# Joined score matmuls in chunks 1 to 3, and a new order of all steps, in a transformer block on one core

## The chip, the cores and the metric

The kernel runs on one core of a Trainium2 chip. A core has five engines that work side by side, each through its own queue in order: TensorE (PE, matmuls; its weight loads are shown apart as PEld), VectorE (DVE), ScalarE (ACT), GpSimd (POOL) and SyncE (SP). Here POOL and SP mostly issue DMA transfers. The metric is the device time of one execution in microseconds; lower is better.

## The reference

One transformer block over 2048 positions of width 512 in bf16. The attention has 32 heads of width 16; each position looks at eight keys, at distances 0, 2, ..., 14 behind it. A feed-forward with a gate, ReLU and width 1376 follows.

```python
off = jnp.arange(8) * 2
idx = pos[:, None] - off[None, :]
mask = idx >= 0
kg = k[:, :, idx_c, :]; vg = v[:, :, idx_c, :]
logits = jnp.einsum("bhsd,bhswd->bhsw", q, kg) * Dh ** -0.5
attn = softmax(where(mask, logits, -1e9))
o = jnp.einsum("bhsw,bhswd->bhsd", attn, vg)

h  = x + attention(layernorm(x)) @ wo
gate = layernorm(h) @ W_gate
up = layernorm(h) @ W_up
h2 = h + (gate * (gate > 0) * up) @ W_down
```

## The kernel before

The 2048 positions go in four chunks (0 to 3) of 512, each of four blocks of 128. Per chunk:

- **Layer norm and projections.** DVE takes statistics, DVE or ACT normalizes, PE (or a DMA transposition on SP, L533) transposes each block, ACT copies it out of PSUM (L560, for pairs of blocks; in chunk 0 block 1's copy is DVE's). Twelve groups of four matmuls (L585) give q, k and v; ACT evicts each (L593).
- **Scores.** The channels are laid out so that a score is a product of q with a shifted k, summed over channels. The eight shifts go in two halves of four (`hf` 0 and 1). DVE multiplies q with shifted k (L636; L651 in chunk 0), two products per half, each 128 x 4096, into the buffers `big`. PE then sums over channels with matmuls whose weights have only 32 columns, so that four of them, one for each shift, use the array together (`tile_position`). A half is one PE step, `sc0` or `sc1`, and one PSUM bank: 16 matmuls (L642), or 8 (L694) where DVE has added the two products first (L680: chunk 2's second half and both halves of chunk 3). ACT takes the exponential of each bank (L708).
- **Attention output.** DVE adds the two halves' exponentials (`es`, L740), PE sums them (`den`, L725), ACT makes the reciprocal, DVE scales the exponentials (L752; in chunk 0 it is done at the end). DMAs on SP and POOL spread them over the channels (`bd`, L768). DVE multiplies with shifted v (`mu`, L800; L815 in chunk 0) and sums eight terms: the first fold by an accumulating DMA on POOL (`ta`, L843) except in one case, the others on DVE (`tree`, L803, L837; `om`, L807). PE does the output projection (`wo`, L881), DVE adds it to x (`rs`, L892).
- **Feed-forward.** ACT squares for the variance (L457), DVE normalizes (`hxn`, L510), four DMA transpositions on SP (`htd`, L533), then up and gate groups of four matmuls (L954), ACT evicts (L958, L961), DVE multiplies (`gu`, L982). The last 96 of the 1376 channels go transposed (L921, L927, L931, and a DMA transposition, L940). PE does the down projection in two parts for each block (`dn`, L1005). In chunks 0 and 1 ACT scales the result (L1011), a DMA on POOL adds it into `x_sm` (`oa`, L1034) and SP stores it (`os`, L1037); in chunks 2 and 3 DVE adds (L1013) and SP stores (L1019), the very last store goes from ACT's queue.

All of this is a list of steps. `add` gives each step its engine, an estimated length, the steps it waits for and the buffers it takes. `RANK` holds one number for each step: the steps are placed in the order of these numbers, so they fix the order of every engine's queue. `Plan.order` also estimates when each step starts, from the arrival times `XT` and `WT` of the loads and the lengths (`MM`, `SW`, ...), and takes for each buffer the one that it thinks is free first. What runs on the chip is the queues in that order, with the waits that the data need. The matmuls of one step stand together in PE's queue.

Buffers that matter here: eight PSUM banks for all results of PE, five `big` buffers of 128 x 4096 (a sixth, the place of the q and k weights, once the last projection has read them) for products, spread weights and value products.

The load of the up weights (`ldu`, L315, two halves) waits for a small DVE copy behind chunk 0's attention (`lg`, L861). The gate weights are loaded in `setup` (L349).

Of the kernel before, what the change touches and what calls it, by code (L numbers as in the profile page):

```python
# [8 lines left out]
P = 128  # L9
# [3 lines left out]
ACT = mybir.ActivationFunctionType  # L13
ALU = mybir.AluOpType
# [3 lines left out]
RANK = [  # L18
# [38 lines left out]
]  # L57
# [36 lines left out]
class Plan:  # L94
# [9 lines left out]
    def add(self, key, *a, **k):  # L104
        op = Op(*a, **k)
        op.key = key
        op.seq = len(self.ops)
        if RANK:
            op.prio = RANK[op.seq]
        self.ops.append(op)  # L110
        for b in set(op.take) | set(op.use):
            b.left += 1
        return op
# [88 lines left out]
def kernel(  # L202
# [11 lines left out]
    nc = tc.nc  # L214
# [8 lines left out]
    PADL = 16  # L223
# [6 lines left out]
    LATE = "ud"  # L230
    NAB = 0
    SCALE = DH ** -0.5
# [68 lines left out]
    V = nc.vector  # L301
# [4 lines left out]
    def f_load(n, i):  # L306
        if n == "d":
            lo, hi = (0, 5) if i == 0 else (5, NFF)
            nc.sync.dma_start(
                wd_sb[:, lo:hi, :], B_W_down[lo * P:hi * P, :].rearrange("(ft p) n -> p ft n", p=P))  # L310
            if FTAIL and i:
                nc.sync.dma_start(wd_sb[:FTAIL, NFF, :], B_W_down[NFF * P:F, :])
        else:
            w = B_W_up.rearrange("(dt p) f -> p dt f", p=P)
            nc.sync.dma_start(wgu_sb[:, 2 * i:2 * i + 2, 1, :], w[:, 2 * i:2 * i + 2, :])  # L315

    def setup():
# [30 lines left out]
        nc.sync.dma_start(wo_sb[:], A_wo.rearrange("(p t) f -> p t f", t=NT))  # L348
        nc.sync.dma_start(wgu_sb[:, :, 0, :], B_W_gate.rearrange("(dt p) f -> p dt f", p=P))  # L349


# [15 lines left out]
    add = plan.add  # L367
# [11 lines left out]
    QA, QC = 6, 3  # L379
    XT = (3.45, 3.65, 4.05, 5.3, 7.15, 8.65, 9.0, 9.4, 13.0, 14.5)  # L380
    WT = (8.35, 8.35, 7.0, 10.85, 15.8, 25.5, 19.2, 29.0)
    DMAT = (('h',0,0),('h',0,2),('h',2,0),('h',2,2),('h',3,0),('h',3,2),('h',1,0),('h',1,2),('x',3,0),('x',3,2))
# [7 lines left out]
    MERGE = (0, 1, 2, 3)  # L390

    BCN = 4

    HG = ([[0, 1, 2, 3]],) * 4
    HSP = ()
    XG = ([[0], [1], [2], [3]], [[0, 1, 2, 3]], [[0, 1, 2, 3]], [[0, 1, 2, 3]])
    TMT = (0, 1, 2, 3)
    TTM, DTG, ATE = 0.0825, 0.27, 0.225
    LASTC = (D // 2, 3 * D // 4)
# [4 lines left out]
    MM, TP = 0.2158, 0.056  # L404
    SW = 0.21
    PEL = 0.22
# [22 lines left out]

    fills = [add(("warm", 0), "PE", 5.6, f_warm, [], -500, take=[wb])]  # L430

    def fill(d, k):
# [7 lines left out]
    def layernorm(tk, src, dst_slots, pr, groups, on_act, residual=None):  # L440
# [7 lines left out]
        for grp in groups:  # L448
# [78 lines left out]
            for j0 in range(lo, hi, step):  # L527
# [23 lines left out]

                tev = not residual and tk == 0 and j0 == 1

# [14 lines left out]
    for tk in range(NCK):  # L568
# [51 lines left out]
        kd = {t: kdone[tk, t] for t in range(NT)}  # L620
        kp = {t: kdone.get((tk - 1, t)) for t in range(NT)}
        for hf in range(2):
            sc, ex = Buf(at_s), Buf(ex_s)
# [54 lines left out]
            elif (tk, hf) in PRE:  # L678
# [18 lines left out]

                scd = [add(("sc%d" % hf, tk), "PE", nu * MM + SW, f_sc, [a], apr, take=[sc], use=[prd[0][1]], lat=PEL)]
            elif tk in MERGE:
# [6 lines left out]

            def f_ex(sc=sc, ex=ex):
                nc.scalar.activation(out=ex.t[:], in_=sc.t[:], func=ACT.Exp, scale=SCALE)  # L708

            def f_mk(hf=hf, ex=ex):  # L710
                V.tensor_tensor(out=ex.t[:, 0:PADL], in0=ex.t[:, 0:PADL], in1=mask[:, hf, :],
                                op=ALU.mult)

            a = add(("ex%d" % hf, tk), "ACT", A5, f_ex, scd, apr, take=[ex], use=[sc], lat=AL)
            if tk == 0:
                a = add(("mk%d" % hf, tk), "DVE", DSM, f_mk, [a], apr, use=[ex], lat=DL)
            exs.append(ex)
            exd.append(a)

# [139 lines left out]
        if tk == 0 and LATE:  # L859
            def f_lg(OT=OT):  # L860
                V.tensor_copy(out=wgu_sb[0:1, :, 1, 0:1], in_=OT.t[0:1, :, 0:1])  # L861

            lg = add(("lg", tk), "DVE", 0.08, f_lg, list(oev.values()), apr, use=[OT], lat=0.1)
            for n in LATE:
                for i in range(2):
                    wload[n].append(add(("ld" + n, i), "SP", 0.45 + 0.1 * (n == "d" and i), lambda n=n, i=i: f_load(n, i),
                                        [lg], 0, lat=1.0 + 1.0 * (n == "d" and i), dq=(1.0, 1.74)))
# [227 lines left out]
```

## Time and profile before

| what | us |
|---|---|
| median of three runs | 191.26 |
| lowest and highest run | 191.16, 192.79 |
| span of the profiled execution | 190.2 |
| PE busy in it | 185.1 |
| DVE busy | 150.7 |
| ACT busy | 113.5 |
| POOL busy | 25.2 |

All times in the views are from the start of that span. A matmul's record is longer than its share of PE's time, because matmuls overlap in the array: one of 512 columns is recorded with 379 ns. What a row of PE's timeline costs is read from its start to the start of the next row. The clock granted to PE over the span is 0.998 of full speed. "To landing" is the time from a DMA's issue to the arrival of its data.

### The profile page before, as it was taken

Reading aid. Unit: us, or ns where it says so; the run is one execution under the profiler, and the core shown is the slowest. Engines: PE = TensorE matmul, PEld = TensorE weight load, DVE = VectorE, ACT = ScalarE, POOL = GpSimd, SP = SyncE. Lnnn points to the kernel's source line nnn. Section 1 sums busy time; section 2 is a strip of 40 time slices with the busy share of each in tenths; the row PEclk is TensorE's granted clock in tenths of the full one; section 3 lists DMA queues with packets and bytes.
Section 4 is the critical chain, followed back from the end, with each engine's and each line's share of the span. In section 5 each row is a group of like instructions: output and inputs, shape, how many; then the busy total and the mean of one; then the engine's idle time right before and its main releaser. Section 6 shows DMA issues by size and latency. Waiting matters only on the chain.

```text
span 190.2 us, 3080 instructions
## 1 busy us (share of the span) xinstructions
PE 185.1 (97%) x1127; PEld 95.4 (50%) x1127; DVE 150.7 (79%) x231; ACT 113.5 (60%) x234; POOL 25.2 (13%) x47
## 2 busy tenths in 40 slices
PE   7799999999999999999999999999999999999993
PEld 7676555554444445544344464444454444455453
DVE  5899999999999999999999998998485712114324
ACT  2579999985467945762483795146466713358500
POOL 4000221400000004230033123027000000000000
PEclk9999999999999999999999999999999999999999
DMA  5999364993198858998438798779922211000503
GB/s 182 281 347 370 90 163 87 191 194 59 21 330 177 233 166 153 194 191 182 83 65 152 142 181 186 180 137 166 221 44 55 55 28 59 28 0 0 165 3 110
DMA packets 27743, 26.98 MB, mean 142 GB/s; under 512 B 14704, under 2 KB 23248, under 8 KB 27728
## 3 DMA queue, kind: packets, MB, share of 16 engines
q1 hardware_dynamic: 23696, 15.34, 29.7%
q0 software_dynamic: 3312, 10.49, 28.6%
q10 hardware_dynamic: 720, 0.95, 1.5%
q8 instruction: 9, 0.15, 0.3%
q14 instruction: 6, 0.05, 0.1%
HBM read 8.42 MB, written 2.10 MB: 55 GB/s over the span
## 4 chain that ended last, share of the span: by engine, by line
PE 82%; ACT 11%; DMA 3%; DVE 1%; issue 1%; SPq 0%
PE bank L954 37%; PE bank L1005 20%; PE bank L585 12%; PE bank L881 7%; ACT row L512 5%; DMA x_sm<-in_A_x_dram 3%; PE bank L921 3%; ACT quad L560 2%; ACT vT L593 2%; PE bank L642 2%; ACT quad L593 1%; PE bank L694 1%; ACT kT L593 1%; ACT ex L708 1%; SPq L323 0%
## 5 line engine op out<-in xcount | busy, mean ns | idle before, releaser
L954 PE MATMUL bank<-quad,wgu_sb 128*128 128x512 bf16 x320 | 72.3, 379 | 0.0
L954 PEld LDWEIGHTS <-wgu_sb 128*128 128x128 bf16 x320 | 30.9, 98 | 37.3 <-issue 1.7
L1005 PE MATMUL bank<-wd_sb,gT 128*128 128x512 bf16 (+3 forms) x198 | 39.7, 355 | 0.0
L958 ACT CAST up_sb<-bank 128x512 bf16<-128x512 f32 x40 | 23.1, 591 | 21.0 <-PE bank L954 14.9
L585 PE MATMUL bank<-quad,wqk_sb 128*128 128x512 bf16 (+2 forms) x176 | 30.4, 321 | 0.5 <-DVE quad L558 0.4
L961 ACT ACTIVATE gr<-bank 128x512 bf16<-128x512 f32 x40 | 23.3, 606 | 9.7 <-PE bank L954 8.2
L1005 PEld LDWEIGHTS <-gT 128*128 128x128 bf16 (+1 forms) x198 | 18.5, 98 | 19.7
L982 DVE TENSOR_TENSOR gT<-gr,up_sb 128x1024 bf16<-128x1024 bf16 x20 | 13.6, 686 | 14.4 <-PE bank L1005 7.0
L636 DVE TENSOR_TENSOR big<-quad,kT 128x4096 bf16<-128x4096 bf16 x11 | 24.8, 2279 | 0.0
L585 PEld LDWEIGHTS <-wqk_sb 128*128 128x128 bf16 x176 | 17.1, 113 | 11.4 <-issue 1.1
L800 DVE TENSOR_TENSOR big<-big,vT 128x4096 bf16<-128x4096 bf16 x9 | 20.4, 2281 | 0.0
L843 POOL DMA_DIRECT2D big<-big x13 | 11.6, 965 | 64.3 <-PE bank L954 32.6
L1013 DVE SCALAR_TENSOR_TENSOR row<-bank,iv,x_sm 128x512 bf16<-128x512 f32 (+2 forms) x10 | 6.3, 643 | 13.4 <-PE bank L1005 13.2
L457 ACT ACTIVATE junk<-x_sm,sm 128x512 bf16<-128x512 bf16 x16 | 11.6, 727 | 8.8 <-DVE x_sm L892 8.8
L585 PE MATMUL bank<-quad,wv_sb 128*128 128x512 bf16 x64 | 16.1, 380 | 0.2 <-ACT quad L560 0.2
L881 PE MATMUL bank<-wo_sb,quad 128*128 128x512 bf16 x64 | 15.0, 379 | 0.0
L892 DVE SCALAR_TENSOR_TENSOR x_sm<-x_sm,bank 128x512 bf16<-128x512 bf16 x16 | 10.8, 678 | 2.4 <-PE bank L881 2.4
L803 DVE TENSOR_TENSOR big<-big 128x1024 bf16<-128x1024 bf16 (+1 forms) x17 | 10.3, 622 | 1.6 <-DMA big<-big 1.4
L467 DVE BATCH_NORM_STATS2 st<-x_sm 128x6 f32<-128x512 bf16 x16 | 10.2, 679 | 1.1 <-DMA x_sm<-in_A_x_dram 1.1
L593 ACT CAST quad<-bank 128x512 bf16<-128x512 f32 x16 | 9.3, 594 | 2.5 <-PE bank L585 2.4
L593 ACT CAST kT<-bank 128x512 bf16<-128x512 f32 x16 | 9.3, 596 | 1.9 <-PE bank L585 1.0
L593 ACT CAST vT<-bank 128x512 bf16<-128x512 f32 x16 | 9.1, 610 | 2.1 <-PE bank L585 2.1
(80 smaller groups left out, 175.6 us busy)
## 6 DMA issues: line engine op xcount, KB each, us to landing
big<-big POOLq DMA_DIRECT2D x13, 512.0 KB, 5.2
big<-ex SPq DMA_DIRECT2D x20, 128.0 KB, 3.1
big<-ex POOLq DMA_DIRECT2D x12, 128.0 KB, 3.8
wgu_sb<-in_B_W_gate_dram SPq DMA_DIRECT2D x1, 1376.0 KB, 9.3
wgu_sb<-in_B_W_up_dram SPq DMA_DIRECT2D x2, 688.0 KB, 5.0
wd_sb<-in_B_W_down_dram SPq DMA_DIRECT2D x2, 640.0 KB, 5.7
x_sm<-in_A_x_dram SPq DMA_DIRECT2D x2, 512.0 KB, 6.2
wqk_sb<-wqk_sb POOLq DMA_DIRECT2D x2, 512.0 KB, 5.8
```

Source lines behind the costliest of these rows:

```text
L457: nc.scalar.activation(out=junk[:, j % 2, :], in_=h.t[:] if h else x_sm[:, tk * BPC + j, :], func=ACT.Square, bias=sm.t[:, j:j + 1], scale ...
L585: nc.tensor.matmul(mm.t[:, lo:hi], lhsT=wv_sb[:, dt, t:D:NT] if c == 2 else wqk_sb[:, dt, c * D + t:(c + 1) * D:NT], rhs=xnT.t[:, dt, lo:h ...
L593: nc.scalar.copy(out=o, in_=mm.t[:])
L636: V.tensor_tensor(out=pb.t[:].rearrange("p (t w) s -> p t w s", t=2), in0=q4, in1=k4, op=ALU.mult)
L800: V.tensor_tensor(out=mt.t[:], in0=ab.t[:], in1=v8, op=ALU.mult)
L843: nc.gpsimd.dma_start(mt.t[:, 0:4, :], mt.t[:, 4:8, :], accum_op=ALU.add)
L881: nc.tensor.matmul(od.t[:], lhsT=OT.t[:, t, j * P:(j + 1) * P], rhs=wo_sb[:, t, :], start=(t == 0), stop=(t == NT - 1 and tk not in RPE))
L954: nc.tensor.matmul(mm.t[:fs, lo:hi], lhsT=wgu_sb[:, dt, g, ft * P: ft * P + fs], rhs=hnT.t[:, dt, lo:hi], start=(dt == 0), stop=(dt == NT ...
L958: nc.scalar.copy(out=ub.t[:fs, i, :], in_=um.t[:fs, :])
L961: nc.scalar.activation(out=gr.t[:fs, i, :], in_=gm.t[:fs, :], func=ACT.Relu)
L982: V.tensor_tensor(out=gt.t[:fs, 0:n, :], in0=gr.t[:fs, 0:n, :], in1=ub.t[:fs, 0:n, :], op=ALU.mult)
L1005: nc.tensor.matmul(od.t[:, c0:c1], lhsT=gts[ft].t[:fs, ft % 2, j * P:(j + 1) * P], rhs=wd_sb[:fs, ft, c0:c1], start=(ft == 0), stop=(ft == ...
```

## The change

In chunks 1, 2 and 3 the two score steps become one (`scB` below, key `sc1`): all matmuls of the first half, then all of the second, into two banks, once the products of both halves are there. The two exponentials stay two steps, and are listed behind it. There are three steps fewer, and `RANK` is a new list of 742 numbers. Of the planner's figures, `SW` goes from 0.21 to 0.19 and some arrival times in `XT` and `WT` change. The gate weights' load can now be a step of its own, if "g" is in `LATE`; `LATE` stays "ud". Which block of chunk 0 DVE copies out of PSUM is now written as `TEV = (1,)`, the block it was.

```diff
 RANK = [
...
 ]
...
+        elif n == "g":
+            nc.sync.dma_start(wgu_sb[:, :, 0, :], B_W_gate.rearrange("(dt p) f -> p dt f", p=P))
...
-        nc.sync.dma_start(wgu_sb[:, :, 0, :], B_W_gate.rearrange("(dt p) f -> p dt f", p=P))
-
+        if "g" not in LATE:
+            f_load("g", 0)
...
-    XT = (3.45, 3.65, 4.05, 5.3, 7.15, 8.65, 9.0, 9.4, 13.0, 14.5)
-    WT = (8.35, 8.35, 7.0, 10.85, 15.8, 25.5, 19.2, 29.0)
+    XT = (3.5, 3.7, 4.6, 6.3, 7.3, 8.3, 8.6, 8.95, 13.1, 14.5)
+    WT = (7.95, 7.95, 6.2, 11.2, 15.8, 25.5, 19.2, 29.0)
...
+    MS = (1, 2, 3)
+    TEV = (1,)
...
-    SW = 0.21
+    SW = 0.19
...
+        both = []
...
-                scd = [add(("sc%d" % hf, tk), "PE", nu * MM + SW, f_sc, [a], apr, take=[sc], use=[prd[0][1]], lat=PEL)]
+                if tk in MS:
+                    both.append((sc, ex, [a], [prd[0][1]], nu, f_sc))
...
+            elif tk in MS:
+                both.append((sc, ex, [a for a, _, _ in prd], [b for _, b, _ in prd], 4, lambda p=prd: [f() for _, _, f in p]))
...
+            if tk in MS and hf == 0:
+                continue
+            if tk in MS:
+                a = add(("sc1", tk), "PE", sum(x[4] for x in both) * MM + SW, lambda p=both: [x[5]() for x in p],
+                        [d for x in both for d in x[2]], apr, take=[x[0] for x in both], use=[d for x in both for d in x[3]], lat=PEL)
+                scs = [(h, x[0], x[1], [a]) for h, x in enumerate(both)]
+            else:
+                scs = [(hf, sc, ex, scd)]
```

The new numbers in `RANK` move steps on every engine. The parts of the queues around the joined runs and around the places that are spoken of below, read from the two lists (`2:q3` is chunk 2's group 3 of q, `up7` and `gt7` are up and gate groups, `pr0_2` the second product of the first half, `pa` the addition of two products, `mmT` the last 96 channels):

```text
PE, chunk 0's output projection to its first up group
before  2:v2 3:k1 2:q3 0:wo2 0:wo0 0:wo3 0:wo1 1:sc1 2:k3 3:k2 1:den 3:q1 2:q2 2:v0 3:v3 3:k0 0:up0
        (1:sc0 stands ahead of 2:v2)
after   2:q2 0:wo1 0:wo0 0:wo3 1:scB 2:v1 0:wo2 3:k0 3:v0 1:den 3:k3 3:v1 2:v2 0:up7

PE, chunk 2's and chunk 3's scores
before  0:gt4 2:sc0 2:sc1 0:gt6          0:dn0b 3:sc0 1:gt6 ... 1:up7 3:sc1 1:gt3
after   0:up3 2:scB 0:up2                1:gt7 3:scB 1:up7

DVE, chunk 0's last sums to chunk 1's first value product
before  0:om3 1:pr1_0 lg 0:rs0 0:rs2 0:hxn0 0:rs3 0:hxn2 0:rs1 0:hxn3 0:hxn1 1:es 2:pr1_0 1:am0 1:am1
        2:pr0_0 2:pr1_2 2:pr0_2 2:pa1 1:mu1
after   0:om3 1:pr1_0 lg 0:rs1 0:rs0 0:hxn1 0:rs3 0:hxn0 2:pr1_0 0:hxn3 0:rs2 1:es 0:hxn2 2:pr0_0
        1:am0 1:am1 2:pr1_2 2:pr0_2 2:pa1 0:gu3 1:mu2

DVE, the opening of chunk 0 (st, ag: statistics; xn: normalize; tv: copy of block 1)
before  st0 ag0 st1 ag1 xn0 st2 xn1 ag2 st3 ag3 tv1 xn2 xn3
after   st0 ag0 st1 ag1 st2 xn0 ag2 xn1 st3 ag3 xn2 tv1 xn3

PE, chunk 2's transpositions (tp) and what stands between them
before  2:tp2 2:tp3 3:v2 3:q3 2:tp1 2:tp0 3:q0 3:k3 0:den 3:v1 2:q0
after   2:tp1 3:v2 2:tp2 2:tp3 3:q1 2:tp0 3:k2 3:q2 2:q3

SP
before  0:ldu0 0:ldu1 0:htd0 0:htd2 0:htd3 0:htd1 1:bd0 1:bd1 0:ldd1 0:ldd0 2:bd0 0:gtd 1:htd1 ...
after   0:ldu0 0:htd1 0:ldu1 0:htd0 0:htd3 0:htd2 1:bd0 1:bd1 0:ldd1 0:ldd0 0:gtd 1:htd1 1:htd0 1:htd3 1:htd2 2:bd0 ...

POOL, the end
before  3:bd0 3:ta2 1:oa3 1:oa1 3:ta0 3:ta1
after   3:bd0 1:oa1 1:oa3 3:ta1 3:ta2 3:ta0

PE and ACT, chunk 1's closing parts of the down projection (o: ACT's scaling)
before  PE dn1b dn3b dn2b dn0b    ACT o3 o1 o2 (square) o0
after   PE dn3b dn0b dn1b dn2b    ACT o3 o0 o1 (square) o2
```

Of chunk 2's up and gate groups, before 16 stand ahead of the first output projection of chunk 3 in PE's queue, after it 17.

More of the change, by code (lines that the diff above doesn't have):

```diff
@@ L430 @@
     fills = [add(("warm", 0), "PE", 5.6, f_warm, [], -500, take=[wb])]
+    if "g" in LATE:
+        wload["g"].append(add(("ldg", 0), "SP", 0.45, lambda: f_load("g", 0), wload["o"], 0, lat=1.0, dq=(1.0, 3.6)))
     def fill(d, k):
@@ L550, in layernorm @@
                 n = len(ds)
-                tev = not residual and tk == 0 and j0 == 1
+                tev = not residual and tk == 0 and j0 in TEV
                 def f_ev(j0=j0, n=n, tp=tp, tev=tev):
@@ L696, in f_sc @@
                                              stop=(u == nu - 1), tile_position=(0, g * HB))
-                scd = [add(("sc%d" % hf, tk), "PE", nu * MM + SW, f_sc, [a], apr, take=[sc], use=[prd[0][1]], lat=PEL)]
+                if tk in MS:
+                    both.append((sc, ex, [a], [prd[0][1]], nu, f_sc))
+                else:
+                    scd = [add(("sc%d" % hf, tk), "PE", nu * MM + SW, f_sc, [a], apr, take=[sc], use=[prd[0][1]], lat=PEL)]
+            elif tk in MS:
+                both.append((sc, ex, [a for a, _, _ in prd], [b for _, b, _ in prd], 4, lambda p=prd: [f() for _, _, f in p]))
             elif tk in MERGE:
@@ L705, with f_ex, f_mk @@
                                    take=[sc], use=[pb], lat=PEL))
[L707 to L718, printed above, removed]
+            if tk in MS and hf == 0:
[4 more added lines that the diff above has]
+                scs = [(h, x[0], x[1], [a]) for h, x in enumerate(both)]
+            else:
+                scs = [(hf, sc, ex, scd)]
+            for h, sc, ex, scd in scs:
+                def f_ex(sc=sc, ex=ex):
+                    nc.scalar.activation(out=ex.t[:], in_=sc.t[:], func=ACT.Exp, scale=SCALE)
+                def f_mk(h=h, ex=ex):
+                    V.tensor_tensor(out=ex.t[:, 0:PADL], in0=ex.t[:, 0:PADL], in1=mask[:, h, :],
+                                    op=ALU.mult)
+                a = add(("ex%d" % h, tk), "ACT", A5, f_ex, scd, apr, take=[ex], use=[sc], lat=AL)
+                if tk == 0:
+                    a = add(("mk%d" % h, tk), "DVE", DSM, f_mk, [a], apr, use=[ex], lat=DL)
+                exs.append(ex)
+                exd.append(a)
         dn, rc = Buf(at_s), Buf(rc_s)
@@ L863 @@
             lg = add(("lg", tk), "DVE", 0.08, f_lg, list(oev.values()), apr, use=[OT], lat=0.1)
-            for n in LATE:
+            for n in LATE.replace("g", ""):
                 for i in range(2):
```

76 rows, old and new, of the table RANK are left out of this document.

## The prediction, made before the change was run

> **What bounds the kernel now.** I read the busy times first, then the list of what TensorE (PE) waited for, then PE's timeline. The page gives busy time, share of the span and instructions by engine:
>
> ```profile
> PE 185.1 (97%) x1127; PEld 95.4 (50%) x1127; DVE 150.7 (79%) x231; ACT 113.5 (60%) x234; POOL 25.2 (13%) x47
> ```
>
> A busy PE need not be PE at its pace, so the waits come next (us in total, times, longest):
>
> ```profile
> PE bank L428 <- DVE warm L327: 1.0, 1, 1.0
> PE bank L544 <- DVE row L515: 0.5, 1, 0.5
> PE bank L585 <- DVE quad L558: 0.4, 1, 0.4
> PE bank L585 <- ACT quad L560: 0.2, 1, 0.2
> ```
>
> The first three are the opening. After it PE waits once. PE's timeline (start, length, line, count) shows where, and how the score runs (L642, L694) sit among the other matmuls:
>
> ```profile
> 37.16 0.38 PE L725 MATMUL bank<-row,spread 128*128 128x512 bf16 x1
> 37.70 1.02 PE L585 MATMUL bank<-quad,wv_sb 128*128 128x512 bf16 x4 [0.16 <-ACT quad L560]
> ```
>
> ```profile
> 43.74 1.03 PE L585 MATMUL bank<-quad,wqk_sb 128*128 128x512 bf16 x4
> 44.69 1.05 PE L642 MATMUL bank<-big,sel 128*32 128x512 bf16 x16
> 45.67 1.05 PE L585 MATMUL bank<-quad,wv_sb 128*128 128x512 bf16 x4
> ```
>
> ```profile
> 48.29 3.62 PE L881 MATMUL bank<-wo_sb,quad 128*128 128x512 bf16 x16
> 51.84 1.05 PE L642 MATMUL bank<-big,sel 128*32 128x512 bf16 x16
> 52.82 1.92 PE L585 MATMUL bank<-quad,wqk_sb 128*128 128x512 bf16 x8
> ```
>
> ```profile
> 59.10 8.80 PE L954 MATMUL bank<-quad,wgu_sb 128*128 128x512 bf16 x40
> 67.83 1.05 PE L642 MATMUL bank<-big,sel 128*32 128x512 bf16 x16
> 68.70 0.60 PE L694 MATMUL bank<-big,sel 128*32 128x512 bf16 x8
> 69.24 1.90 PE L954 MATMUL bank<-quad,wgu_sb 128*128 128x512 bf16 x8
> ```
>
> ```profile
> 94.83 11.38 PE L954 MATMUL bank<-quad,wgu_sb 128*128 128x512 bf16 x52
> 106.14 0.61 PE L694 MATMUL bank<-big,sel 128*32 128x512 bf16 x8
> 106.69 2.76 PE L954 MATMUL bank<-quad,wgu_sb 128*128 128x512 bf16 x12
> ```
>
> ```profile
> 127.31 11.38 PE L954 MATMUL bank<-quad,wgu_sb 128*128 128x512 bf16 x52
> 138.53 0.82 PE L921 MATMUL bank<-wgu_sb,quad 128*128 128x192 bf16 x8
> ```
>
> ```profile
> 142.53 1.90 PE L881 MATMUL bank<-wo_sb,quad 128*128 128x512 bf16 x8
> ```
>
> The pace of one matmul of 512 columns is (138.53 - 127.31) / 52 = 0.2158 us. Start to start, almost every row above is its count at that pace: PE's queue is full and in order, and the time is what stands in that queue. The change keeps every matmul, so it can win only what is not matmul (the turns into and out of the score runs, the wait at 37.70), and lose wherever the new order makes PE wait. Work on the other engines is the same too; only its place moves.
>
> **The change part by part.** *The score runs.* Four score matmuls share the array, so 16 of them are worth 4 x 0.2158 = 0.863 and 8 are worth 0.432.
> - Chunk 1, first half: the four matmuls ahead of it take 44.69 - 43.74 = 0.95, 0.09 over their pace, and the run 0.98, 0.12 over. Turn: 0.21.
> - Chunk 1, second half: 51.84 - 48.29 = 3.55 for 16, 0.10 over; the run 0.98, 0.12 over. Turn: 0.22.
> - Chunk 3, second half: 106.14 - 94.83 = 11.31 for 52, 0.09 over; the run 0.55, 0.12 over. Turn: 0.21.
> - Chunk 2: its halves stand next to each other already. From 67.83 to 68.70 is 0.87 for 16: no turn between them.
>
> So a joined run pays one turn, as chunk 2 shows, and the change removes one turn in chunk 1 and one in chunk 3, none in chunk 2: 2 x 0.215 = 0.43 us. [...] The gates between the halves are DVE's: the joined run waits for the second half's products too. In the new DVE order these end before PE arrives (chunk 1's last product is the step before the small copy that frees the up loads, as before), so I cost that wait at nothing; uncovered it would be up to one product, 2.2.
>
> *The wait at 37.70.* From 37.16 to 37.70 PE does one matmul of 0.22, so 0.32 is lost, waiting for ACT's copy of a transposition. In the new order chunk 3's projections are spread between chunk 2's transpositions, but the same copies still end close to where PE needs them. Bounds: gain 0.32, or nothing. I take 0.2.
>
> *The opening.* DVE now does block 2's statistics before it normalizes block 0, which puts the first transposition later by one statistics step, while the next things PE needs still wait for block 3's data. I take 0, bounds -0.3 and +0.3, less than the 0.5 and 0.4 waits of the opening shown above.
>
> *The feed-forward of chunk 0.* Here three queues move: on DVE a product of 2.2 us (chunk 2's) and the 0.4 sum of chunk 1's exponentials now stand ahead of the last normalization; on SP the second load of the up weights stands behind the first DMA transposition; all of it gates PE's first up run. The rows (DVE first, then SP, then "to landing" for the up loads and for the last three transpositions):
>
> ```profile
> 48.20 2.28 DVE L636 TENSOR_TENSOR big<-quad,kT 128x4096 bf16<-128x4096 bf16 x1
> ```
>
> ```profile
> 53.96 0.40 DVE L740 TENSOR_TENSOR row<-ex,ex 128x512 bf16<-128x512 bf16 x1
> ```
>
> ```profile
> 50.59 0.90 SPq L315 DMA_DIRECT2D wgu_sb<-in_B_W_up_dram  x2
> 52.05 5.25 SPq L533 DMA_TRANSPOSE quad<-row  x4
> ```
>
> ```profile
> DMA to landing us min/median/max: 4.3/5.0/5.7
> ```
>
> ```profile
> DMA to landing us min/median/max: 2.6/3.5/4.3
> ```
>
> Before, all four normalizations are done at 53.96. Now add 2.2 and 0.34: the last is done at 56.5, and its transposition, issued at 56.6, lands 2.6 to 4.3 later, at 59.2 to 60.9. PE gets to its first up run after one more projection group (0.863) less chunk 1's saved turn (0.21), at 59.10 + 0.65 = 59.75, or 59.55 with the 0.2 above. The second up load, issued near 53.1, lands by 58.8 at 5.7. Bounds: no wait, or 1.35. The transposition goes late enough to run mostly alone, like the last one before (2.6), so I take 0. The denominator of chunk 1, which now stands 2.8 ahead of that up run on PE, needs the sum that DVE ends at 56.3; PE gets there at 56.8: 0. The broadcasts of chunk 1's weights follow on SP, before from 57.48 (the row counts those that a window to 62 holds, of eight):
>
> ```profile
> 57.48 4.46 SPq L768 DMA_DIRECT2D big<-ex  x7
> ```
>
> ```profile
> big<-ex SPq DMA_DIRECT2D x20, 128.0 KB, 3.1
> ```
>
> Now DVE's scalings end behind one more product, at 59.1, so the eighth goes at 59.1 + 7 x 0.64 = 63.6 and lands at 66.7. DVE wants it for chunk 1's first value product after three more products' time and one gate-up product, at 59.4 + 6.6 + 0.6 = 66.6. I take 0; the bound is 0.5.
>
> *The output projection of chunk 3.* On POOL the two additions of chunk 1's result into x_sm now stand ahead of all three accumulates of chunk 3 (before, one accumulate had gone first). The rows: POOL (the second addition and the accumulates behind it), the landing of chunk 3's three accumulates (the first of them issued earlier), SP, DVE:
>
> ```profile
> 129.61 0.85 POOL L1034 DMA_DIRECT2D x_sm<-up_sb  x1 [0.40 <-ACT up_sb L1011]
> 130.15 2.07 POOL L843 DMA_DIRECT2D big<-big  x2
> ```
>
> ```profile
> DMA to landing us min/median/max: 4.7/6.2/10.3
> ```
>
> ```profile
> 131.70 0.38 SPq L1037 DMA_DIRECT2D out_dram<-x_sm  x1
> ```
>
> ```profile
> 140.99 0.69 DVE L803 TENSOR_TENSOR big<-big 128x1024 bf16<-128x1024 bf16 x1 [0.80 <-DMA big<-big]
> 141.72 0.76 DVE L837 TENSOR_TENSOR quad<-big 128x512 bf16<-128x512 bf16 x2
> ```
>
> Before, the last accumulate is there at 140.99, DVE ends the sums at 142.48 and PE starts the projection at 142.53, without a wait but without slack. Now PE closes block 3 of chunk 1 first, the one that ACT scales first, so the additions go about 1.2 earlier (one closing part of 3 x 0.2158 and the turns saved). One more accumulate follows them. Two of chunk 1, issued 0.69 apart with no store beside them, landed at 75.6 and 78.2, that is 2.6 apart (the second line's range is these two):
>
> ```profile
> 70.98 0.85 POOL L843 DMA_DIRECT2D big<-big  x1 [32.59 <-PE bank L954]
> 71.67 1.04 POOL L843 DMA_DIRECT2D wqk_sb<-wqk_sb  x1
> ```
>
> ```profile
> DMA to landing us min/median/max: 4.6/5.5/6.5
> ```
>
> The pair from 130.15 on landed 4.6 apart (6.2 and 10.3, half a us between the issues), with the store of 131.70 beside it: the store costs 2.0. So the last of three lands at 140.99 - 1.2 + 2.6 = 142.4, at 144.4 if the added one costs 4.6, and at 140.4 if the store stays clear of them. DVE's three last sums take 0.6 + 2 x 0.34 = 1.3; PE could start at 143.7, 145.7 or 141.7. It arrives after one more up or gate group, less the 0.43, less the 0.2: 142.53 + 0.863 - 0.63 = 142.77. The wait is 0.9, with the bounds 0 and 2.9. I take 0.4, about half way between the case without the store and the one with it: the store is released by the second addition as before, but whether its packets fall among three accumulates as among two no row tells.
>
> *The rest.* Load of the gate weights: same call, same place, since "g" is not in LATE. Arrival times, SW and TEV feed the planner alone; through it they choose which buffer a step gets. I cost that at nothing; a buffer chosen badly costs a wait like those above. The tail (last matmul to last store) ends in the same two steps, DVE and ACT's store: 0.
>
> **Sum.** On the profiled execution: -0.43 - 0.2 + 0.4 = -0.23, from a span of 190.2 to 190.0. The median of the runs is 191.26, 1.06 over the span for what lies around it. So 191.26 - 0.23 = 191.0.
>
> **The rivals.**
> - *The accumulates decide (slower).* The store falls on them with its full price: a wait of 1.9 at chunk 3's output projection, the middle of 0.9 to 2.9. It decides as soon as the last accumulate lands after 141.5 (142.77 less 1.3). For it: one more accumulate in the same queue, and DVE already waited 0.8 for the last one. Against: the additions go earlier. Time: 191.26 - 0.63 + 1.9 = 192.5. [...]
> - *Chunk 0's first up run waits.* The last transposition takes 4.3 as when the up loads were beside it: wait 1.35. Time: 191.26 - 0.63 + 0.4 + 1.0 = 192.0 (1.0, since it may share in part). For it: the loads now overlap the transpositions longer. Against: the last one of before took 2.6.
> - *All covers hold.* No wait at 142.77, the whole 0.32 and up to 0.3 in the opening won: 191.26 - 0.43 - 0.32 - 0.3 = 190.2.
> - *The joining saves nothing*, because the second half's products come late to it: 191.26 - 0.2 + 0.4 = 191.5.
>
> **How the numbers follow.** Chances: the forecast 0.45, the accumulates 0.2, chunk 0's up run 0.1, all covers 0.15, nothing saved 0.05, and 0.05 for several waits together, 193 and more. The range leaves out that last case and reaches a little beyond the slower rivals: low 190.2, high 192.7. About 1% (1.9 us) is what a measurement of this kernel can tell from no change. All named cases lie within it; only waits that add up (0.1 with the upper ends of both rivals) pass 193.2. Faster by 1% would need 1.9, and turns and waits that could go are 0.43 + 0.32 + 0.3: 0.02. So faster 0.02, same 0.88, slower 0.10.
>
> **What would show it.** PE's timeline of the new kernel should have one L642 run of 32 in chunk 1, some 1.85 long from start to start, one L694 run of 16 in chunk 3, 0.98, and nothing new in chunk 2. The list of PE's waits should show nothing near the first up run of chunk 0; a wait of L954 for a DMA there proves the second rival. A wait of PE at L881 near 143 for DVE, with DVE at L803 waiting for a DMA before it, is the first rival, and its length prices the 0.4. The wait for ACT's copy at L560 should be shorter than 0.32. The forecast is wrong if PE's last matmul moves by more than 1 us either way, or if any wait over 0.5 stands at another place.

## The result, and the profile after

The changed kernel took 198.66 us (median of four runs, 198.20 to 198.84), beside 191.41 for the kernel before on the same chip: a ratio of 1.0366, 95% interval 1.0324 to 1.0407. It is slower by 3.7%. The profiled execution took 198.2 with a span of 196.3; before, the span was 190.2. In two of the tests below one slow run each (200.43 and 203.0 us) is left out of the median and the ratio.

Line numbers move: the score runs are now L651 and L703, products L645, up and gate groups L977, the down projection L1028, the output projection L904, `mu` L823, `tree` L826 and L860, the spread weights L791, the transpositions of a chunk L541 and of its tail L963.

The page of the changed kernel, busy time by engine:

```profile
PE 184.8 (94%) x1108; PEld 95.5 (49%) x1127; DVE 150.4 (77%) x231; ACT 114.4 (58%) x234; POOL 25.2 (13%) x47
```

No engine does much more work (ACT 0.9 us more, the others no more than before). What PE waited for, in the changed kernel (us in total, times, longest):

```profile
PE bank L977 <- DMA quad<-row: 3.5, 2, 2.6
PE bank L552 <- DVE row L523: 1.3, 2, 1.0
PE bank L433 <- DVE warm L329: 1.0, 1, 1.0
PE bank L977 <- ACT gr L984: 0.8, 1, 0.8
PE bank L904 <- DVE quad L860: 0.6, 1, 0.6
```

Where that is shows in the view by windows, cut at the first up or gate run of chunks 0, 1 and 2 (length, then busy time and count by engine; granted clock, DMA share). The changed kernel:

```profile
0.00:60.28 60.28, 57.45 (x445) 34.78 (x452) 56.71 (x106) 45.32 (x88) 7.81 (x24) 1.00 0.72 187
60.28:96.03 35.75, 34.43 (x182) 15.88 (x186) 34.88 (x41) 22.63 (x49) 5.62 (x8) 1.00 0.70 153
96.03:133.51 37.48, 33.33 (x171) 15.14 (x175) 32.44 (x40) 19.60 (x41) 9.18 (x13) 1.00 0.72 149
```

The kernel before, cut at the same runs:

```profile
0.00:59.10 59.10, 56.92 (x447) 34.11 (x448) 56.18 (x105) 43.89 (x85) 7.81 (x24) 1.00 0.71 191
59.10:94.83 35.73, 35.72 (x199) 16.52 (x198) 35.48 (x42) 21.92 (x47) 5.65 (x8) 1.00 0.80 175
94.83:127.31 32.48, 32.48 (x165) 15.09 (x166) 31.48 (x40) 18.23 (x40) 8.27 (x11) 1.00 0.71 145
```

PE's idle time is length less busy: 2.8, 1.3 and 4.2 after, 2.2, 0.0 and 0.0 before. From chunk 2's first up group on the two kernels take the same (62.79 and 62.89). So the loss lies ahead of it, most of it between 96 and 133.5. The same rows show that DVE was nearly full up to there: before, it was busy for 35.48 of 35.73 and 31.48 of 32.48 us, after for 34.88 of 35.75 and only 32.44 of 37.48. Its 79% over the whole span hides that. PE's timeline of the changed kernel names the places (start, length, count, idle before and its releaser):

```profile
52.15 1.91 PE L651 MATMUL bank<-big,sel 128*32 128x512 bf16 x32
53.99 1.05 PE L593 MATMUL bank<-quad,wv_sb 128*128 128x512 bf16 x3
...
96.03 1.89 PE L977 MATMUL bank<-quad,wgu_sb 128*128 128x512 bf16 x8 [0.91 <-DMA quad<-row]
...
107.14 0.61 PE L703 MATMUL bank<-big,sel 128*32 128x512 bf16 x8
107.58 0.60 PE L703 MATMUL bank<-wqk_sb,sel 128*32 128x512 bf16 x8
108.12 1.04 PE L977 MATMUL bank<-quad,wgu_sb 128*128 128x512 bf16 x4
109.97 5.34 PE L977 MATMUL bank<-quad,wgu_sb 128*128 128x512 bf16 x23 [0.81 <-ACT gr L984]
...
121.54 3.32 PE L904 MATMUL bank<-wo_sb,quad 128*128 128x512 bf16 x13 [0.61 <-DVE quad L860]
...
133.51 4.48 PE L977 MATMUL bank<-quad,wgu_sb 128*128 128x512 bf16 x19 [2.58 <-DMA quad<-row]
```

The joined runs have the lengths that were forecast: 53.99 - 52.15 = 1.84 in chunk 1, 108.12 - 107.14 = 0.98 in chunk 3. The largest wait, 2.58, is for chunk 2's DMA transpositions. They go through SP; its queue in the changed kernel:

```profile
88.58 5.12 SPq L541 DMA_TRANSPOSE quad<-row  x4
93.86 3.64 SPq L791 DMA_DIRECT2D big<-ex  x4
101.61 0.41 SPq L1060 DMA_DIRECT2D out_dram<-x_sm  x1
120.27 3.55 SPq L791 DMA_DIRECT2D big<-ex  x4
123.91 2.82 SPq L963 DMA_TRANSPOSE gT<-row  x1
126.83 5.15 SPq L541 DMA_TRANSPOSE quad<-row  x4
```

and in the kernel before:

```profile
81.70 4.18 SPq L768 DMA_DIRECT2D big<-ex  x4
85.98 1.26 SPq L940 DMA_TRANSPOSE gT<-row  x1
88.33 5.12 SPq L533 DMA_TRANSPOSE quad<-row  x4
114.75 3.94 SPq L768 DMA_DIRECT2D big<-ex  x4
118.78 0.55 SPq L1037 DMA_DIRECT2D out_dram<-x_sm  x1
119.43 1.26 SPq L940 DMA_TRANSPOSE gT<-row  x1
120.79 5.15 SPq L533 DMA_TRANSPOSE quad<-row  x4
```

The new order puts chunk 3's weighting of the exponentials (`am`) late on DVE. Its spread weights, next in SP's queue, go out at 120.27 and not at 114.75, and chunk 2's transpositions start at 126.83 and not at 120.79. Their input is DVE's normalization of the first block; the changed kernel, then the kernel before:

```profile
123.03 0.35 DVE L518 TENSOR_SCALAR row<-x_sm,sm 128x512 bf16<-128x512 bf16 x1
```

```profile
119.53 0.35 DVE L510 TENSOR_SCALAR row<-x_sm,sm 128x512 bf16<-128x512 bf16 x1
```

In the changed kernel the block was there at 123.38 and its transposition went 3.45 later, behind the spread weights and chunk 1's tail (`gT`, 2.82) in SP's queue. Before, it was there at 119.88 and went 0.91 later. So of the 6.0 us, 2.5 are SP's queue and 3.5 are the block itself, which DVE had later.

Chunk 2's spread weights moved as well, from 81.70 to 93.86, and DVE waits for them (changed kernel, DVE's timeline):

```profile
101.99 2.29 DVE L823 TENSOR_TENSOR big<-big,vT 128x4096 bf16<-128x4096 bf16 x1 [2.36 <-DMA big<-ex]
```

From this came two theories: that the order, by its late softmax tails (sum, denominator, reciprocal, weighting, spread weights), carries the loss, and that the joining does.

### The profile page after: what moved, and what is told of

The parts are those of the page before. It is cut to its first block, busy times and chain, and to the rows that moved or that the text cites. A ratio compares the mean times of both kernels' runs of the same rounds, so it can differ in the third digit from the quotient of the medians.

```text
span 196.3 us, 3056 instructions
## 1 busy us (share of the span) xinstructions
PE 184.8 (94%) x1108; PEld 95.5 (49%) x1127; DVE 150.4 (77%) x231; ACT 114.4 (58%) x234; POOL 25.2 (13%) x47
## 4 chain that ended last, share of the span: by engine, by line
PE 46%; DVE 23%; DMA 15%; issue 10%; POOL 3%; SPq 1%; POOLq 0%; DVEq 0%
PE bank L977 20%; PE bank L593 10%; PE bank L1028 10%; DMA big<-ex 7%; DVE big L660 4%; PE bank L904 4%; DVE big L823 4%; DMA x_sm<-in_A_x_dram 3%; DMA big<-big 3%; DVE st L475 3%; DMA quad<-row 3%; DVE big L645 2%; DVE big L826 2%; PE bank L944 1%; POOL big L791 1%
## 5 line engine op out<-in xcount | busy, mean ns | idle before, releaser
L977 PE MATMUL bank<-quad,wgu_sb 128*128 128x512 bf16 x312 | 72.1, 379 | 4.7 <-DMA quad<-row 3.5
L977 PEld LDWEIGHTS <-wgu_sb 128*128 128x128 bf16 x320 | 30.9, 98 | 41.6 <-issue 6.6
L1028 PE MATMUL bank<-wd_sb,gT 128*128 128x512 bf16 (+3 forms) x194 | 39.7, 355 | 0.3
L984 ACT ACTIVATE gr<-bank 128x512 bf16<-128x512 f32 x40 | 24.0, 608 | 19.5 <-PE bank L977 14.4
L593 PE MATMUL bank<-quad,wqk_sb 128*128 128x512 bf16 (+2 forms) x172 | 29.7, 320 | 0.5 <-DMA quad<-row 0.2
L1028 PEld LDWEIGHTS <-gT 128*128 128x128 bf16 (+1 forms) x198 | 18.4, 98 | 19.7 <-DMA gT<-row 0.3
L823 DVE TENSOR_TENSOR big<-big,vT 128x4096 bf16<-128x4096 bf16 x10 | 22.5, 2287 | 3.5 <-DMA big<-ex 3.5
L645 DVE TENSOR_TENSOR big<-quad,kT 128x4096 bf16<-128x4096 bf16 x11 | 24.9, 2282 | 0.0
L904 PE MATMUL bank<-wo_sb,quad 128*128 128x512 bf16 x63 | 15.7, 379 | 0.7 <-DVE quad L860 0.6
L593 PE MATMUL bank<-quad,wv_sb 128*128 128x512 bf16 x62 | 15.5, 379 | 0.1
L826 DVE TENSOR_TENSOR big<-big 128x1024 bf16<-128x1024 bf16 (+2 forms) x19 | 11.9, 658 | 2.7 <-DMA big<-big 2.6
L791 POOL DMA_DIRECT2D big<-ex x12 | 6.8, 582 | 42.4 <-DVE ex L775 20.5
L904 PEld LDWEIGHTS <-quad 128*128 128x128 bf16 x64 | 6.1, 98 | 9.1 <-DVE quad L860 1.9
L601 ACT CAST kT<-bank 128x512 bf16<-128x512 f32 x16 | 9.5, 591 | 1.3 <-PE bank L593 0.8
```

The lines of the kernel that those rows point to most:

```text
L593: nc.tensor.matmul(mm.t[:, lo:hi], lhsT=wv_sb[:, dt, t:D:NT] if c == 2 else wqk_sb[:, dt, c * D + t:(c + 1) * D:NT], rhs=xnT.t[:, dt, lo:h ...
L645: V.tensor_tensor(out=pb.t[:].rearrange("p (t w) s -> p t w s", t=2), in0=q4, in1=k4, op=ALU.mult)
L823: V.tensor_tensor(out=mt.t[:], in0=ab.t[:], in1=v8, op=ALU.mult)
L826: V.tensor_tensor(out=mt.t[:, 0:n, :], in0=mt.t[:, 0:n, :], in1=mt.t[:, n:2 * n, :], op=ALU.add)
L904: nc.tensor.matmul(od.t[:], lhsT=OT.t[:, t, j * P:(j + 1) * P], rhs=wo_sb[:, t, :], start=(t == 0), stop=(t == NT - 1 and tk not in RPE))
L977: nc.tensor.matmul(mm.t[:fs, lo:hi], lhsT=wgu_sb[:, dt, g, ft * P: ft * P + fs], rhs=hnT.t[:, dt, lo:hi], start=(dt == 0), stop=(dt == NT ...
```

## The experiments

Every time below is a median, with the ratio to the kernel before on the same chip (whose median was 192.0 to 192.2 there). The ratio is an estimate of its own and need not be the quotient of the two medians. The diffs show the queues, since the edit of each is new numbers in `RANK`.

### The joining alone, and the order alone

```diff
 the kernel before, PE
-1:sc0 2:v2 3:k1 2:q3 0:wo2 ... 0:wo1 1:sc1      0:dn0b 3:sc0 1:gt6 ... 1:up7 3:sc1
+      2:v2 3:k1 2:q3 0:wo2 ... 0:wo1 1:scB      0:dn0b       1:gt6 ... 1:up7 3:scB
```

> The kernel before, its order of all steps and its constants, with the joining alone: in chunks 1 to 3 the score product runs once, at the place of its second half, and the first exponential stands right before the second. Theory (the joining is sound, the new order costs the time): the run of chunk 1 takes about 1.84 us and that of chunk 3 about 0.98, as in the changed kernel, one pair of turns of 0.21 is saved in chunks 1 and 3, and the time is 190.8 to 191.2 us, a ratio of 0.997 to 1.000. Rival A (the joining itself costs: products held longer, the exponentials bunched behind one run): the time comes out 2 us or more above the kernel before, 193 to 198.7.

Measured: 192.57, ratio 1.0022 (0.9997 to 1.0046). Rival A falls: the joining is not what costs 7 us. But the saving isn't there either. PE's timeline of this kernel shows why:

```profile
48.66 3.63 PE L904 MATMUL bank<-wo_sb,quad 128*128 128x512 bf16 x16 [1.23 <-DVE quad L830]
52.22 1.91 PE L651 MATMUL bank<-big,sel 128*32 128x512 bf16 x32
```

Before, the first half's run stood ahead of that output projection and covered DVE's last products of chunk 0's attention. Joined, it stands behind it, and PE waits 1.23 instead.

```diff
 the changed kernel, MS = (), PE
-2:k3 2:q0 2:v0 2:k2 2:q2 ... 1:scB       1:up3 ... 3:scB
+2:k3 1:sc0 2:q0 2:v0 2:k2 2:q2 ... 1:sc1 1:up3 3:sc0 ... 3:sc1
```

> The changed kernel's order with the halves of the scores in runs of their own again: chunk 1's first half five projection groups ahead of its second, chunk 3's first half some nine groups ahead, chunk 2's side by side. Theory (the new order alone carries the loss): 198.4 to 199.6, that is at the changed kernel's 198.66 or up to 0.9 above it, two pairs of turns at 0.21 more. Rival A (the joining carries it): under 195.

Measured: 198.27, ratio 1.0320 (1.0266 to 1.0373), 0.13 under the range. Without any joining the new order is about as slow as the change. That settles which part of the change costs.

### The softmax tails of chunks 2 and 3

```diff
 the changed kernel (chunk 2's tail earlier)
 ACT  2:ex0 +2:ex1 ... -2:ex1
 DVE  0:gu2 +2:es ... 0:guT0 +2:am1 +2:am0 ... -2:es ... -2:am1 -2:am0
 SP   0:gtd +2:bd0 1:htd1 1:htd0 1:htd3 1:htd2 -2:bd0
```

> The changed kernel with one group of steps moved: chunk 2's second exponential, sum of exponentials, denominator, logarithm and reciprocal, the two weightings and the issue of its spread weights stand earlier, so that the spread weights are issued some 8 us earlier. Theory (late softmax tails cost the time): VectorE's wait of 2.4 us before chunk 2's first multiplication, the wait of 0.81 for an activation slot and the 0.61 before chunk 2's output projection shrink or go, and the time is 1.5 to 3 us under the changed kernel's 198.66: 195.7 to 197.2. Rival B (the opening's 0.58 and the later waits for the transpositions carry it alone): 198 to 199.

Measured: 198.41, ratio 1.0365 (1.0311 to 1.0418). The theory missed, and the time is in the range of rival B: DVE no longer waits for chunk 2's spread weights, the waits of 0.81 and 0.61 are gone, and nothing clear of the noise is won. PE's timeline:

```profile
95.83 2.43 PE L977 MATMUL bank<-quad,wgu_sb 128*128 128x512 bf16 x8 [2.60 <-issue]
...
132.66 4.48 PE L977 MATMUL bank<-quad,wgu_sb 128*128 128x512 bf16 x19 [2.15 <-DMA quad<-row]
```

PE came to chunk 1's first gate group at 95.83 - 2.60 = 93.23, 1.9 earlier than in the changed kernel (96.03 - 0.91 = 95.12), and began it only 0.2 earlier (1.4 of the 1.9 had come with an earlier first up group of chunk 0, at 58.88). The view names no releaser for the 2.60 ("issue"). But chunk 1's transpositions now stand behind the moved spread weights in SP's queue: the first goes at 89.17, the last at 93.3, and with the 2.5 to landing that the last one took in the kernel before (an estimate for this one) it is there at 95.8, where PE begins. Before chunk 2's first up group PE still waits 2.15.

```diff
 the changed kernel (chunk 3's tail earlier)
 DVE  +3:es 1:gu0 ... 1:gu2 +3:am1 +3:am0 ... 2:tree1_1 -3:am1 -3:am0
 SP   +3:bd1 0:os3 -3:bd1 1:gtd 2:htd0
```

> The changed kernel with the other group moved: chunk 3's sum of exponentials, denominator, logarithm, reciprocal and weightings stand earlier, its spread weights are issued on SP some 5 us earlier, and the transposition of chunk 1's tail moves ahead of the weighting with them. Theory (SP's queue, held by the spread weights of chunk 3, holds chunk 2's transpositions): the 2.58 us that PE waits before chunk 2's first up group goes to under 0.5, and the time is 2 to 3 us under the changed kernel: 195.7 to 196.7. Rival C (the transpositions are late because VectorE's output of chunk 2 is late, whatever SP holds): the wait stays over 1.5 and the time within 1 us of 198.66.

Measured: 195.31, ratio 1.0171 (1.0123 to 1.0220), 3.35 under the changed kernel (by the ratios 3.7): more than expected, though a wait of 1.23 is left in the profiled run (its slowest of four, 196.82). SP's queue and PE's timeline there:

```profile
94.14 27.49 SPq L791 DMA_DIRECT2D big<-ex  x8
121.72 1.88 SPq L1060 DMA_DIRECT2D out_dram<-x_sm  x1
123.70 1.92 SPq L963 DMA_TRANSPOSE gT<-row  x1
125.72 5.15 SPq L541 DMA_TRANSPOSE quad<-row  x4
```

```profile
132.21 2.96 PE L977 MATMUL bank<-quad,wgu_sb 128*128 128x512 bf16 x13 [1.23 <-DMA quad<-row]
```

The spread weights are earlier (the row of eight holds chunk 2's four and chunk 3's), but now a store takes 1.88 right ahead of the transpositions.

Both groups together:

> Both groups of steps moved earlier in the changed kernel, chunk 2's and chunk 3's. Theory: the gains add, 4 to 5.5 us under the changed kernel, 193.2 to 194.7; what is left over the kernel before is then the opening (0.58), the 1.1 at chunk 1's first gate group and small ones, less the 0.43 saved. Rival D (the two cover one another: the first wait removed is only made up at the second): the time is that of the better single move within 0.7.

Measured: 195.99, ratio 1.0196 (1.0157 to 1.0236). The gains don't add; rival D held. PE waits 2.22 before chunk 1's first gate group, much as with chunk 2's tail alone, and 0.86 before chunk 2's first up group.

The converse, chunk 3's spread weights behind the transpositions:

```diff
 the changed kernel
 SP   -3:bd1 1:gtd 2:htd0 2:htd2 2:htd3 2:htd1 +3:bd1
```

> The changed kernel with one issue moved on SP: chunk 3's second set of spread weights (with the first multiplication that reads it) stands behind chunk 2's transpositions instead of ahead of them. Theory (SP's queue in order holds the transpositions): PE's 2.58 before chunk 2's first up group falls to under 0.7, and as the spread weights now come some 5 us later, a new wait of 3 to 6 stands before chunk 3's output projection, which had 1.5 of slack: 198.5 to 202. Rival C (VectorE's late output sets the transpositions): the 2.58 stays over 1.5.

Measured: 200.88, ratio 1.0449 (1.0406 to 1.0492). As the theory has it: no wait is left before chunk 2's first up group (rival C falls), and DVE waits for the spread weights:

```profile
133.29 8.90 DVE L823 TENSOR_TENSOR big<-big,vT 128x4096 bf16<-128x4096 bf16 x4 [8.00 <-DMA big<-ex]
```

PE pays for that 4.12 at 146.18, not quite at chunk 3's output projection but a group ahead of it, for a bank that DVE frees (L954).

### The store, and chunk 2's tail placed as before

```diff
 the changed kernel with chunk 3's tail earlier
 SP   3:bd1 -0:os3 1:gtd 2:htd0 2:htd2 2:htd3 2:htd1 +0:os3
```

> Chunk 3's softmax tail earlier as in the second test of this study's tails, and besides the store of chunk 0's block 3 (1.9 us on SP between the spread weights and the transposition of chunk 1's tail) behind chunk 2's transpositions. Theory (each issue ahead of the transpositions in SP's queue counts): the wait before chunk 2's first up group (1.2 there) goes to under 0.5, and the time falls by 0.5 to 1.2 from 195.31, to 194.1 to 194.8. Rival C (the blocks on VectorE set the transpositions by then): 195 to 195.7.

Measured: 194.26, ratio 1.0131 (1.0098 to 1.0164): the wait went to 0.25 and the time where it was expected. Of the 7.25 us lost, moving chunk 3's tail and one store gives back 4.4 (198.66 - 194.26; by the ratios, 1.0366 to 1.0131, 4.5).

```diff
 the changed kernel, chunk 3's tail and the store as above, and
 DVE  1:mu1 +2:es ... 0:gu2 +2:am1 +2:am0
 POOL 1:ta0 +2:bd1 1:ta1
 SP   0:ldd1 +2:bd0 0:ldd0 0:gtd 1:htd1
```

> As with both groups earlier, but chunk 2's softmax tail stands earlier still (its sum of exponentials right after chunk 1's second multiplication), so that SP issues its spread weights before chunk 0's tail transposition and chunk 1's four transpositions find them out of the way; the store of chunk 0's block 3 stands behind chunk 2's transpositions. Theory (whatever stands in SP's queue right ahead of a chunk's transpositions delays its first up or gate group): the wait before chunk 1's first gate group (2.60 with both groups earlier) goes to under 0.5 and that before chunk 2's first up group (1.24) to under 0.6, and the time is 191.7 to 193.2. Rival (VectorE's and the accumulates' load sets the waits, wherever the issues stand): over 194.5.

Measured: 209.33, ratio 1.0874 (1.0832 to 1.0915), far off, by where the edit put two issues. (The 2.60 and 1.24 that the expectation gives for both groups earlier are near the waits of the two single moves, 2.60 and 1.23; with both it was 2.22 and 0.86.) SP held the second load of the down weights behind the spread weights until 86.10, and PE waited for it:

```profile
94.91 6.26 PE L1028 MATMUL bank<-wd_sb,gT 128*128 128x512 bf16 x16 [12.77 <-DMA wd_sb<-in_B_W_down_dram]
```

On POOL the last accumulate of chunk 1 went at 84.16, behind the spread weights, and DVE waited 8.64 for it. With both issues behind what they had held:

```diff
 SP   0:ldd1 -2:bd0 0:ldd0 +2:bd0 0:gtd 1:htd1
 POOL 1:ta0 -2:bd1 1:ta1 +2:bd1
```

> As the last version with both groups earlier, but with the two issues put right that held others there: chunk 2's spread weights stand on SP behind the second load of the down weights (which they had held for 12.8 us), and on POOL behind the last accumulate of chunk 1. Theory (what stands ahead of a chunk's transpositions in SP's queue sets the loss): the waits before chunk 1's first gate group and before chunk 2's first up group go to under 0.5 each, the time is 192.0 to 193.6, some 2 to 3.5 us under both groups earlier (195.99). Rival (VectorE's and the accumulates' load sets the waits wherever the issues stand): over 194.5.

Measured: 194.00, ratio 1.0106 (1.0077 to 1.0135). SP's queue and PE's waits, profile of this kernel:

```profile
81.29 3.64 SPq L791 DMA_DIRECT2D big<-ex  x4
...
114.32 4.42 SPq L791 DMA_DIRECT2D big<-ex  x4
...
121.88 5.15 SPq L541 DMA_TRANSPOSE quad<-row  x4
```

```profile
94.66 1.89 PE L977 MATMUL bank<-quad,wgu_sb 128*128 128x512 bf16 x8 [0.32 <-issue]
...
128.43 4.48 PE L977 MATMUL bank<-quad,wgu_sb 128*128 128x512 bf16 x20 [0.48 <-DMA quad<-row]
```

Both waits are under 0.5 as expected, and the time is 0.4 above its range, though under the rival's 194.5. Its interval overlaps that of the version with chunk 2's tail left late (1.0131), so chunk 2's late tail can't be shown to cost anything by itself.

### What the joining lost

```diff
 the kernel before with the joining alone, PE
-2:q3 0:wo2 0:wo0 0:wo3 0:wo1 1:scB 2:k3 3:k2
+2:q3 2:k3 0:wo2 0:wo0 0:wo3 0:wo1 1:scB 3:k2
```

> The kernel before with the joining alone, and one projection group of chunk 2 (4 matmuls, 0.86 us) moved from behind the joined run of chunk 1 to ahead of chunk 0's output projection. Theory (joined, the first half's run no longer covers VectorE's last products of chunk 0's attention, so the output projection waits 1.2 us): that wait falls to 0.3 or less, the time is 0.6 to 0.9 us under the joining alone, 191.6 to 192.0, at or just under the kernel before. Rival (the 0.4 lost by the joining alone stands elsewhere, at the exponentials or the buffers): 192.3 to 192.8, as without the move.

Measured: 193.06, ratio 1.0054 (1.0030 to 1.0078): it missed. The wait fell only to 0.46, a second one of 0.39 came for a bank that the moved group holds (it ends with ACT's copy of k, L601), and PE waited 0.72 before chunk 1's first gate group. One group isn't free cover here.

```diff
 the kernel before, joined with MS = (2, 3), PE
-0:dn0b 3:sc0 1:gt6 ... 1:up7 3:sc1
+0:dn0b       1:gt6 ... 1:up7 3:scB
```

> The kernel before with the runs of chunks 2 and 3 joined and chunk 1's left apart. Theory (chunk 1's joining takes away the run that covered VectorE's last products of chunk 0's attention; chunk 3's saves its pair of turns): no wait of 1.2 before chunk 0's output projection, and 0.2 us under the kernel before, ratio 0.997 to 1.0005, under the 1.0022 of all three joined. Rival (chunk 3's joining costs as well): ratio over 1.001.

Measured: 192.76, ratio 1.0038 (1.0008 to 1.0067). The first part held: with chunk 1's halves apart the wait before chunk 0's output projection is 0.20. The second didn't: there is still a loss and no gain. Chunk 2's joining is in this test too and was not run alone; PE's timeline puts the loss at chunk 3's. This kernel:

```profile
94.80 11.38 PE L977 MATMUL bank<-quad,wgu_sb 128*128 128x512 bf16 x52 [0.81 <-issue]
```

and of the kernel before:

```profile
94.21 0.62 PE L694 MATMUL bank<-big,sel 128*32 128x512 bf16 x8
94.83 2.53 PE L954 MATMUL bank<-quad,wgu_sb 128*128 128x512 bf16 x11
```

The gate group starts at 94.8 in both. Before, chunk 3's first half filled the 0.62 ahead of it; joined, that time is part of a wait of 0.81, and the work is done later. The view names no releaser here either; the last of chunk 1's transpositions goes at 92.2, and with 2.5 to landing, the median of this kernel's transpositions, it is there at about 94.7. Last, the covers moved with no joining at all:

```diff
 the kernel before, PE
-1:sc0 2:v2 3:k1 2:q3 0:wo2 0:wo0 ... 0:dn0b 3:sc0 1:gt6
+2:v2 3:k1 2:q3 0:wo2 1:sc0 0:wo0 ... 0:dn0b 1:gt6 3:sc0
```

> The kernel before with no joining at all, every run and both its turns kept: only the two first-half runs are moved a little later, chunk 1's (0.98 us) from ahead of chunk 0's output projection to behind its first group, and chunk 3's (0.62) from ahead of chunk 1's first gate group to behind it. Theory (what the joining lost is the cover of these two runs: PE waits there for VectorE's last products and for chunk 1's transpositions whatever it does): waits of 0.5 to 1.2 before chunk 0's output projection and of 0.5 to 0.9 before chunk 1's first gate group appear, and the time is 0.3 to 1.2 us over the kernel before, 192.4 to 193.3. Rival (the joining itself costs, by the products it holds or the exponentials behind it): no such waits, 191.8 to 192.3.

Measured: 194.05, ratio 1.0097 (1.0066 to 1.0128), beyond the range expected. PE's timeline:

```profile
48.16 1.04 PE L881 MATMUL bank<-wo_sb,quad 128*128 128x512 bf16 x4 [1.29 <-DVE quad L807]
49.12 1.05 PE L642 MATMUL bank<-big,sel 128*32 128x512 bf16 x16
50.95 2.75 PE L881 MATMUL bank<-wo_sb,quad 128*128 128x512 bf16 x12 [0.78 <-ACT ex L708]
```

The first wait is the one that the joining alone had (1.23). The 0.78 is new: PE waits for a bank until an exponential on ACT (L708) is done, which this place adds. Before chunk 1's first gate group only 0.25 shows, since PE comes there late by then. The cover of chunk 1's run is shown; that of chunk 3's rests on the test with chunks 2 and 3 joined.

## Why the prediction was wrong

The forecast was 191.0, the result 198.66, outside the range; the case that came true is the one that it gave 0.05, several waits together, but at other places than those that it had priced.

**The step that failed** is the list of moves that were priced. The prediction priced the new order at chunk 0's feed-forward and at chunk 3's output projection, and put the rest at 0. The softmax tails of chunks 2 and 3 moved too, by 12 and by 5.5 us on SP, and with chunk 3's tail everything behind it in SP's queue: the transposition of chunk 1's tail and chunk 2's four. That was never worked out. In its place the runs show 2.58 of wait, and 4.4 us given back when chunk 3's tail and one store are put out of the way. The issue on SP that waited held all that was behind it: SP stood from 102.0 to 120.27 for DVE's weighting (a wait of 18.2 for L775), and issued nothing else in that time.

The standing alone cost nothing in the kernel before: SP stood even longer there for the same weighting, 21.2 us up to 114.75, but chunk 2's first block was only there at 119.88. What cost time in the changed kernel is that it ended so late that the issues behind it were still going out when the block was there (3.45 and not 0.91 from block to transposition, a difference of 2.5 beside PE's wait of 2.58).

The prediction's first reading, that the time is what stands in PE's queue, leaves DVE out. Up to 127.31 DVE was busy for 123.1 us in the kernel before, so a step that moves later on DVE or in a queue that feeds it has little slack to move in.

**The score runs.** Their lengths were right (1.84 and 0.98). What failed is that 2 x 0.215 of PE's time would be time of the kernel. Both first halves stood just ahead of a place where PE would otherwise wait. The joining gave 1.0022 (three chunks) and 1.0038 (two), not 0.998.

**The joined run's wait for the second half's products**: none, as costed. The products were not the cover to look at; the run itself was.

**The wait at 37.70** (0.2 won): gone in the changed kernel, another of 0.18 stands at 33.65.

**The opening** (0, bounds 0.3): the first up run began 1.18 later; 0.65 of it was forecast. But in five other profiles of kernels with this opening it began at 58.88, 59.21, 59.57, 60.35 and 61.40, so one profile can't settle it.

**Chunk 0's first up run** (0, rival 1.35): no wait in this profile, in which PE came there late. The last transposition took 2.8 to land, where the prediction took 2.6 and the rival 4.3. But in five of the eight other profiles of kernels with this opening PE waits there 0.32 to 0.75 for a transposition, 0.72 with chunk 3's tail earlier. So this rival was right in kind and too dear.

**Chunk 1's first value product** (0, bound 0.5): DVE waited 0.76 for the spread weights (at 68.17), more than the bound; before, it did not wait there.

**Chunk 3's output projection** (0.4, rival 1.9): no wait; PE came there 7 us later than before, so the case wasn't put to the test.

**The sum.** The waits of 0.91, 0.81, 0.61 and 2.58 are 4.9 of the 6.1 us between the spans. PE's idle time up to the first up run is 0.6 more than before (2.8 against 2.2); the other 0.6 is spread over small gaps.

**What stays open.** The best version of the new order is still 1.1% over the kernel before. PE's waits in that version after the opening are some 1.9 us in all, 0.7 of them at chunk 2's denominator; which moves cause those wasn't tried. Nor was it taken apart why DVE had chunk 2's first block 3.5 us later in the changed kernel. No version that beats the kernel before was found.

## What to carry to other kernels

Before a saving on the busiest engine is counted, look at what stands right behind the saved work: if the next step starts when a transfer lands, the saved time can turn into a wait (here chunk 1's first gate group started at 94.83 behind a run of 0.62, and at 94.80 behind a wait of 0.81 with that run joined). With a new order, go through each in-order queue, DMA-issuing ones first, and for every issue that moved later ask what stands behind it and when that could have gone. A queue of cheap issues (SP in the changed kernel, by the median 0.40 us for a store of `os`, 0.56 for one of the spread weights, 1.2 for a transposition) can hold a matmul queue, when one of them waits: here for 12.77 us, in the version with the held load. And before a saving on the busiest engine is counted, look at the second one stage by stage: DVE's 79% was 97% up to 127 us.

## What was not expected

Chunk 1's first gate group starts between 94.65 and 96.35 in the profiles of all kernels here but the one with the held load, while PE's arrival there moves by nearly 3 us (from 93.23 with chunk 2's tail earlier to 96.06 with the covers moved). At that point the chain of DVE, SP and the transpositions sets the time as much as PE does, although PE's busy share before was 97% and its list of waits showed nothing there: the run of 0.62 that stood in front hid it. In the kernel before the last of chunk 1's transpositions goes at 92.3 and takes 2.5 to land, at about 94.8, and the gate group starts at 94.83.
